# Chunked attention with a channel mix on one core: 1 KB rows for refetched weights, stores of pairs on another queue, a new order of all steps

## The chip, the cores and the metric

The kernel runs on one core of a Trainium2 chip. The metric is device time in microseconds of that core for one execution. TensorE multiplies, VectorE and ScalarE work on tiles in between, and DMAs are issued from the queues of SyncE (SP), ScalarE and GpSimd (POOL). A page of the hardware profiler and its trace belong to the kernel.

## What is computed

Attention runs in chunks of 64 rows within a sequence of 576, for 8 batches and 8 heads of width 64. Its result goes through a channel mix: each row is blended with the row before it by two vectors, and two matrix products with a squared ReLU between them are gated by a sigmoid.

```python
scores = scale * np.matmul(q_c, k_c.transpose(0, 1, 2, 4, 3))
attn = np.exp(scores - np.max(scores, axis=-1, keepdims=True))
out = np.matmul(attn / (np.sum(attn, axis=-1, keepdims=True) + 1e-09), v_c)
...
xk = mu_k * x + (1.0 - mu_k) * x_prev
xr = mu_r * x + (1.0 - mu_r) * x_prev
k = np.maximum(xk @ w_k, 0.0)
v = k * k @ w_v
r = 1.0 / (1.0 + np.exp(-(xr @ w_r)))
return (r * v).astype(np.float32)
```

There are 8 x 576 = 4608 rows of 512 channels; `w_k` is 512 x 1024, `w_v` 1024 x 512, `w_r` 512 x 512, all float32.

## The kernel before

The 4608 rows are cut into 18 groups of 256 rows, and each group into two tiles of 128. For each tile t the kernel loads q, k and v, brings q and k into a form with channels on partitions, and multiplies the scores (steps `S`, line 714). VectorE and ScalarE make the softmax (`S` or, from group 3 on, `Z` for a whole group), TensorE transposes it and multiplies with v (steps `P`, lines 831 and 844). The first three groups are loaded in natural rows (`load_nat`, lines 459 and 476) and turned on TensorE (`T`, lines 639 and 663). From group 3 on `load_blocks` (lines 519 and 521) fetches blocks of 32 x 32 (four DMAs for a step such as `bk11.2`), and VectorE transposes within them (`D`, line 689). `load_v` (line 491) takes four DMAs a tile.

The channel mix multiplies float32 values as a high and a low part, three passes each. The gates `R` (line 1130) take twelve matmuls of 512 columns a tile. Groups 0 to 3 multiply directly (`K`, line 1084, and `V`, line 1163). From group 4 on two groups form a pair (pairs 2 to 8) and go through a scheme with seven products of blocks instead of eight: `M` (line 1396, fourteen series of twelve matmuls of 256 columns) for the first product, `V1` to `V7` (line 1486, as many) for the second. ScalarE and VectorE move the results out, add them (`C`, line 1410), square them (`E`) and split them into high and low parts (`F`, line 1440); `O` (lines 1500 and 1504) adds and gates the second product, and `Q` stores a tile (line 1150).

The scheme needs sums of weights. Those of `w_v` (`tv`, eight pieces of 512 KB in sum form) and the split gate weights `wr` (four pieces) are made once, written to a buffer `kept` in HBM (lines 1282 and 1299), and fetched again for each of the pairs 3 to 8, because their places in SBUF are used for other tiles in between. `load_pair_weights` does that from POOL's queue: steps `L` (line 1308 for `tv`, line 1319 for `wr`), twelve DMAs of 512 KB a pair, each a row of 4 KB on each of 128 partitions.

Nothing is scheduled at run time. The functions only record named steps. `ORDER`, a table of 2089 words, lists the steps in the order in which they are issued, with the engine behind a colon where there is a choice (`:A` ScalarE, `:D` VectorE); `PLACE` gives every tile its offset in one of two arenas in SBUF or its bank in PSUM. The framework adds a semaphore wait wherever a step reads or overwrites what another engine or a DMA still works on. Each engine and each queue runs its own steps strictly in this order, so a step that waits holds all behind it on its engine. Eight semaphores serve the DMAs of each kind of queue in turn: a DMA of POOL also waits until the one eight before it has landed. SP issues everything but the refetches.

Of the kernel before, what the change touches and what calls it, by code (L numbers as in the profile page):

```python
# [19 lines left out]
G = 256  # L20
# [3 lines left out]
W.0:D swr1.0 cwr1.1:A cwr1.0:A W.1 nk0.0 nq0.0 mu.0 nk0.1 nq0.1 nq1.0 swk1.0 nk1.0 v0.0 v1.0 swr0.0  # L24
nk2.0 T0.6 T0.8:D mu.1 T0.0 mu.2:A T0.7:A cwr1.2:D T0.1:A T0.2:D T0.3 T0.9 S0.0 cwr1.3:D T0.11:D
T0.10:A T0.5:A T0.4:A S0.1:D S1.0 S0.2:D S1.1:D S1.2:D S0.3:A S0.4:D S0.5:D P0.3:D hwr1.0:A T1.0
P0.0 T1.3 cwk1.1:A S1.3:A P0.1:A cwk1.0:A S1.4:D S1.5:D P0.2 P0.4:D cwk1.2:D hwr1.1:D cwk1.3:D P1.0
T1.4:A T1.2:A P1.1:A T1.1:A dg.2 dg.3 Mr0.0 P1.2 S2.0 T1.5:A S3.0 T2.3 cwr0.1:A cwr0.0:A T2.5:A
T2.4:A hwk1.0:A P1.3:D Mr0.1:D P1.4:D Ak9.0:D S2.1:D cwr0.2:D Mr0.2:D cwr0.3:D S2.2:D Mr1.0 hwr0.0:A
nq2.0 T2.0 swk3.0 T2.1:A S2.3:A cwk3.0:A S3.1:D hwr0.1:D S3.2:D S3.3:A T2.2:A hwk1.1:D Mr1.1:A  # L30
cwk3.1:A dg.1 dg.0 Mk0.0 S2.4:D R00.0 Mk1.0 P2.3:D S3.4:D S2.5:D P2.0 S3.5:D Mr1.2:D cwk3.2:D
R00.1:A Mk0.1:A cwk3.3:D P2.1:D v3.0 v2.0 swk2.0 swk0.0 kr.0 cwk2.0:A cwk2.1:A P3.0 P3.1:A R01.0
cwk2.2:D Mk1.1:D hwk3.0:A hwk3.1:D Mk1.2:D cwk2.3:D P2.2 S4.0 P3.2 S5.0 P2.4:A R01.1:A cwk0.0:A
cwk0.1:A Mr2.0 hwk2.0:A Mr2.1:A Mk0.2:D cwk0.2:D S5.1:D Mk2.0 swv3.0 cwv3.0:A P3.3:D P3.4:A Mk2.1:A
hwk2.1:D Mr2.2:D cwk0.3:D Mk3.0:D K01.0 R10.0 bk4.3 swv2.0 bk4.0 swv1.0 bk4.1 hwk0.0:A K01.1:A
Mk2.2:D S4.1:D Mk3.1:D hwk0.1:D cwv3.1:A Mk3.2:D cwv3.2:D K03.0 K03.1:A R10.1:A cwv1.0:A K01.2:A
Mr3.0:D K00.0 K02.0 cwv3.3:D K01.3:A hwv3.0:D Mk3.3:D hwv3.1:D Mr3.1:D cwv1.1:A K00.1:D swv0.0
K00.2:A cwv0.0:A K03.2:A cwv1.2:D K01.4:D cwv1.3:D K13.0 K12.0 cwv0.1:A K03.3:D Mr3.2:D cwv0.2:D
cwv2.1:A cwv2.0:A cwv2.2:D cwv0.3:D bk4.2 K02.1:A K02.2:A hwv1.0:A hwv1.1:D R11.0 K00.3:A hwv0.0:A
K00.4:D hwv0.1:D S5.2:D D8.1:D Ar2.0:D K03.4:D K10.0 R11.1:A cwv2.3:D K10.1:A K13.1:A S5.3:A K02.3:A  # L40
K11.0 K02.4:D S4.2:D hwv2.0:D K13.2:D hwv2.1:D K10.2:A V01.0 V00.0 V01.1 V00.1 K13.3:D Ak2.0:D
S5.4:D V00.2 V01.2 V01.3 V01.4 V00.3 V01.5 V01.6 V01.7 V00.4 K10.3:A S4.3:A K11.1:A S4.4:D S4.5:D
K11.2:A K11.3:A K12.1:A K11.4:D S5.5:D K10.4:D P4.0 V00.5 V00.6 P5.0 V11.0 V00.7 V11.1 V10.0 V11.2
V11.3 U0.2:D U1.2:D U0.0:D bq4.0 bq3.2 bq3.3 bq3.0 bq3.1 D7.0:D K12.2:D bk3.0 v4.0 bk3.3 bk3.1 bk3.2
v5.0 U0.3:D K13.4:D D6.0:D K12.3:A P4.1:A P5.1:A D6.1:D V01.8:D D7.1:D K12.4:D U0.1:D U0.4:D S6.0
P4.2 P5.2 S7.0 Z3.0:D Ak2.2:A Bk2.1:D Z3.1:D V11.4 V10.1 Ak2.1:A Z3.2:A A2.0:A Hk12.0:A V00.8:D
# [294 lines left out]
def tile_chunk_attention_channel_mix(  # L341
# [76 lines left out]
    def queue(e):  # L418
        return nc.scalar if e == "A" else nc.sync
# [1197 lines left out]
```

## Time and profile before

| | |
|---|---|
| time, median of 3 runs | 666.2 us (665.04 to 672.01) |
| the profiled execution | 667.85 us |
| its span, first to last instruction | 666.0 us |
| mean granted clock of TensorE | 0.944 |
| DMA traffic | 93.35 MB, 139 GB/s over the span |

The profiled execution's own time stands 1.85 us above its span: what lies around the first and last instruction. In the rows below, times are microseconds from the start of the span unless marked ns. The number in brackets at the end of a timeline row is the idle time of the engine just before that row, and behind the arrow stands what ended it. DMA rows give the count, the size of one and the median time from issue to landing.

### The profile page before, as it was taken

How to read it: one execution, taken by the hardware profiler on the slowest of the kernel's cores; microseconds unless marked ns; L12 is line 12 of the kernel's file. 1: busy time of each engine (PE TensorE's matmuls, PEld its weight loads, DVE VectorE, ACT ScalarE, POOL GpSimd, SP SyncE). 2: the span in 40 equal slices, each digit the busy share in tenths (PEclk: the TensorE clock that was granted, in tenths of full speed). 3: DMA queues.
4: the chain of work that ended last, by engine and by line, in shares of the span. 5: the costliest groups of instructions: out<-in, count | busy, mean ns of one | idle time of the engine just before them, and what ended most of it. 6: DMA issues, size and time to landing. Idle time of an engine off the chain costs nothing. (4 is left out here: it accounts for less than half of the span.)

```text
span 666.0 us, 15832 instructions
## 1 busy us (share of the span) xinstructions
PE 589.9 (89%) x6183; PEld 544.3 (82%) x6183; DVE 526.5 (79%) x882; ACT 411.6 (62%) x811; POOL 52.4 (8%) x94
## 2 busy tenths in 40 slices
PE   6689899799988999879986959969998979999997
PEld 4578888688868998779875959959887879999897
DVE  4677799859798999779856857769879778998684
ACT  4486574545875996677644836547855846686451
POOL 4300000000000020002100201001100210011000
PEclk8789999979989999989997979979999979999999
DMA  9777532433344388536934675635746957233601
GB/s 244 170 197 225 154 66 51 109 75 58 101 99 81 85 276 237 140 76 169 295 58 115 154 178 160 179 62 135 222 87 169 246 163 181 78 127 84 234 1 64
DMA packets 200123, 93.35 MB, mean 140 GB/s; under 512 B 178024, under 2 KB 181104, under 8 KB 200048
## 3 DMA queue, kind: packets, MB, share of 16 engines
q1 hardware_dynamic: 189680, 54.58, 36.6%
q0 software_dynamic: 10368, 37.75, 17.2%
q8 instruction: 49, 0.80, 0.5%
q14 instruction: 26, 0.21, 0.1%
HBM read 76.55 MB, written 15.73 MB: 139 GB/s over the span
## 5 line engine op out<-in xcount | busy, mean ns | idle before, releaser
L1396 PE MATMUL m<-rounded 128*128 128x256 f32 x1176 | 152.0, 289 | 12.5 <-ACT plain L412 4.1
L1486 PE MATMUL o<-rounded 128*128 128x256 f32 x1176 | 153.1, 290 | 8.4 <-DVE rounded L1440 7.1
L1396 PEld LDWEIGHTS m<-rounded 128*128 128x128 f32 x1176 | 147.1, 196 | 15.8 <-ACT plain L412 5.1
L1486 PEld LDWEIGHTS o<-rounded 128*128 128x128 f32 x1176 | 148.4, 197 | 10.7 <-DVE rounded L1440 7.7
L412 ACT ACTIVATE rounded<-plain 128x512 fp32r<-128x512 f32 (+1 forms) x166 | 105.7, 662 | 38.1 <-PE pv L1163 8.4
L1130 PE MATMUL pr<-rounded 128*128 128x512 f32 x432 | 111.6, 412 | 4.0 <-DVE rounded L954 2.0
L1130 PEld LDWEIGHTS pr<-rounded 128*128 128x128 f32 x432 | 84.1, 200 | 22.9 <-DVE rounded L954 2.5
L1440 DVE TENSOR_TENSOR rounded<-plain,rounded 128x512 fp32r<-128x512 f32 x98 | 65.2, 684 | 16.8 <-PE m L1396 5.4
L1007 ACT ACTIVATE plain<-xps,mu 128x256 f32<-128x256 f32 x128 | 54.5, 489 | 30.3 <-PE xps L844 20.6
L689 DVE STREAM_TRANSPOSE plain<-plain 128x512 f32<-128x512 f32 x60 | 41.5, 701 | 34.1 <-DMA plain<-in_q 18.0
L1013 ACT ACTIVATE plain<-xps,mu 128x255 f32<-128x255 f32 (+3 forms) x176 | 62.3, 450 | 0.7 <-PE s L714 0.7
L1308 POOL DMA_DIRECT2D rounded<-kept x48 | 26.3, 554 | 308.8 <-PE o L1486 86.6
L412 ACT ACTIVATE plain<-m 128x512 f32<-128x512 f32 x42 | 24.5, 596 | 41.0 <-DMA out<-plain 14.1
L1024 DVE TENSOR_TENSOR plain<-plain 128x512 f32<-128x512 f32 x64 | 43.0, 680 | 7.0 <-ACT plain L1013 6.7
L1084 PEld LDWEIGHTS pk<-rounded 128*128 128x128 f32 x384 | 47.2, 192 | 1.2 <-ACT plain L1142 0.6
L1084 PE MATMUL pk<-rounded 128*128 128x256 f32 x384 | 47.8, 284 | 0.0
L1163 PE MATMUL pv<-rounded 128*128 128x512 f32 x192 | 47.5, 397 | 0.0
L844 PE MATMUL xps<-plain 64*64 64x64 f32 x1152 | 28.7, 236 | 17.3 <-DMA plain<-in_v 8.8
L844 PEld LDWEIGHTS xps<-plain 64*64 64x64 f32 x1152 | 23.8, 147 | 21.8 <-DMA plain<-in_v 10.9
L1163 PEld LDWEIGHTS pv<-rounded 128*128 128x128 f32 x192 | 35.5, 190 | 7.0
L1410 DVE TENSOR_TENSOR plain<-m,plain 128x512 f32<-128x512 f32 x42 | 28.3, 682 | 14.9 <-ACT plain L412 11.5
L1448 DVE TENSOR_TENSOR plain<-plain 128x512 f32<-128x512 f32 x56 | 38.0, 686 | 0.5
(103 smaller groups left out, 739.0 us busy)
## 6 DMA issues: line engine op xcount, KB each, us to landing
rounded<-kept POOLq DMA_DIRECT2D x72, 512.0 KB, 6.5
plain<-in_v SPq DMA_DIRECT2D x144, 64.0 KB, 2.4
out<-plain SPq DMA_DIRECT2D x36, 256.0 KB, 2.3
kept<-rounded SPq DMA_DIRECT2D x12, 512.0 KB, 2.8
plain<-in_q SPq DMA_DIRECT2D x160, 32.0 KB, 2.0
plain<-in_k SPq DMA_DIRECT2D x160, 32.0 KB, 2.1
plain<-in_moe_w_k SPq DMA_DIRECT2D x4, 1024.0 KB, 6.4
plain<-in_moe_w_v SPq DMA_DIRECT2D x4, 1024.0 KB, 5.7
```

Of the source, the lines that this page charges most:

```text
L412: nc.scalar.activation(to, x, AF.Copy)
L689: nc.vector.transpose(out=x, in_=x)
L844: nc.tensor.matmul(T[f"xps{g}"][halves[c], 2 * j + a, tl * TT + e * CH : tl * TT + (e + 1) * CH], T[f"v{t}"][halves[j], hp, e, :], T[f"pT{ ...
L1007: nc.scalar.activation(now(nm, h)[:, c], xps()[:, cb], AF.Copy, scale=mu2[:, 0, i, cb : cb + 1])
L1013: nc.scalar.activation(before(nm)[:, cb, s : s + n], xps()[:, cb, s - 1 : s - 1 + n], AF.Copy, scale=mu2[:, 1, i, cb : cb + 1],)
L1024: engine[e].tensor_tensor(now(nm, h), now(nm, h), before(nm)[:, 2 * h : 2 * h + 2], ALU.add)
L1084: nc.tensor.matmul(pk[:, e, :], wk_at(f // 4)[:, a, cb, f % 4 * P : (f % 4 + 1) * P], x[:, b, cb, :], start=(n == 0), stop=(n == 3 * NB - 1),)
L1130: nc.tensor.matmul(pr, xr_at(g, a, cb)[:, tl * TT : (tl + 1) * TT], wr_of(g, cb // 2)[:, b, cb % 2, :], start=(n == 0), stop=(n == 3 * NB ...
L1163: nc.tensor.matmul(pv, kk_at(g, a, f // 2)[:, f % 2, tl * TT : (tl + 1) * TT], wv_at(f // 4)[:, :, b, f % 4, :], start=(f == 0 and n == 0) ...
L1396: nc.tensor.matmul(ps[w][:, e, :], left(n, a, cb, 2 * u + e), right(g, n, b, cb), start=first and i == 0, stop=i == 11, skip_group_check=True,
L1440: engine[e].tensor_tensor(form(p, n, u, 1), r(i), f32(form(p, n, u, 0)), ALU.subtract)
L1486: nc.tensor.matmul(ps[w][:, tl, :], form(p, n, u, a)[:, e, tl * TT : (tl + 1) * TT], moving(n, b, 2 * u + e), start=first and i == 0, stop ...
```

## The change

Three things are edited in the code. A refetch of 512 KB is now issued as four DMAs, each of 256 columns, so a row of 1 KB on each of 128 partitions. The stores `Q` of pairs are issued from POOL, and the function `queue` knows POOL. The two tables are drawn anew: all steps are the same, but they stand in another order, some on the other of the two engines they may use, with other places. Twelve of the first loads are marked for ScalarE's queue in the new table.

```diff
     def queue(e):
-        return nc.scalar if e == "A" else nc.sync
+        return {"A": nc.scalar, "G": nc.gpsimd}.get(e, nc.sync)
...
+    def fetch(to, of):
+        for c in range(0, 1024, 256):
+            nc.gpsimd.dma_start(out=to[:, c : c + 256], in_=of[:, c : c + 256])
+
     def load_pair_weights(p):
...
                 def fn(e, n=n, u=u):
-                    nc.gpsimd.dma_start(
-                        out=tv_at(p, n, u).rearrange("p s c n -> p (s c n)"), in_=kept[2 * (n - 4) + u]
-                    )
+                    fetch(tv_at(p, n, u).rearrange("p s c n -> p (s c n)"), kept[2 * (n - 4) + u])
...
                 for h in range(2):
-                    nc.gpsimd.dma_start(out=x[:, 1024 * h : 1024 * (h + 1)], in_=kept[8 + 2 * i + h])
+                    fetch(x[:, 1024 * h : 1024 * (h + 1)], kept[8 + 2 * i + h])
...
                 do.task = f"Q{c}{tl}_{p}"
-                do(store(2 * p + c, tl), "Q")
+                do(store(2 * p + c, tl), "G")
```

Of the table of the order, its first line:

```diff
-W.0:D swr1.0 cwr1.1:A cwr1.0:A W.1 nk0.0 nq0.0 mu.0 nk0.1 nq0.1 nq1.0 swk1.0 nk1.0 v0.0 v1.0 swr0.0
+nq0.0:A nk0.0:A swr1.0 nk0.1:A mu.0 nq0.1:A W.0:D W.1 T0.0 T0.6 T0.2:D P0.3:D T0.1:D T0.8:D T0.7:D
```

**POOL's queue.** The rows below are those from the first refetch on, before the change (`rounded` is the arena that holds the split weights, `kept` the buffer in HBM; line 1319 fetches gate weights, line 1308 sums of `w_v`).

```order
L1319 DMA rounded<-kept 128x1024 x4
L1308 DMA rounded<-kept 128x1024 x7
L1319 DMA rounded<-kept 128x1024 x2
L1308 DMA rounded<-kept 128x1024 x2
L1319 DMA rounded<-kept 128x1024 x2
L1308 DMA rounded<-kept 128x1024 x5
```

After the change POOL has, from its first refetch on (line 1305 is the new `fetch`, line 1150 a store):

```order
L1305 DMA rounded<-kept 128x256 x16
L1150 DMA out<-plain 128x512
L1305 DMA rounded<-kept 128x256 x4
L1150 DMA out<-plain 128x512
L1305 DMA rounded<-kept 128x256 x4
L1150 DMA out<-plain 128x512 x2
L1305 DMA rounded<-kept 128x256 x44
L1150 DMA out<-plain 128x512 x3
```

The four stores of pair 2 now stand between the refetches of pair 3, and the stores of pair 3 behind its last refetch and the first ones of pair 4.

**SP's queue.** Around the loads of k for group 11 (line 519 loads its first 64 rows, line 521 the other 192), before the change:

```order
L491 DMA plain<-in_v 64x4x64 x4
L519 DMA plain<-in_k 32x4x32 x2
L521 DMA plain<-in_k 32x6x32 x4
...
L519 DMA plain<-in_k 32x4x32 x2
L521 DMA plain<-in_k 32x6x32 x4
L1150 DMA out<-plain 128x512
L491 DMA plain<-in_v 64x4x64 x4
L1150 DMA out<-plain 128x512 x2
L521 DMA plain<-in_k 32x8x32 x8
```

And at the same loads after it:

```order
L491 DMA plain<-in_v 64x4x64 x4
L519 DMA plain<-in_k 32x4x32 x2
L521 DMA plain<-in_k 32x6x32 x4
...
L521 DMA plain<-in_q 32x8x32 x12
L519 DMA plain<-in_k 32x4x32 x2
L521 DMA plain<-in_k 32x6x32 x4
L521 DMA plain<-in_q 32x8x32 x4
L491 DMA plain<-in_v 64x4x64 x8
```

The stores are gone from here, and loads for the next group are mixed in earlier.

**The start.** ScalarE's first steps before the change:

```order
L579 ACT_TABLE_LOAD
L579 ACTIVATE plain<-plain 128x1024
L575 ACTIVATE plain<-plain 128x1024
L540 ACTIVATE mu_78<-mu_t 128x8
L541 ACTIVATE mu_78<-mu_t 128x8
```

And after it:

```order
L476 DMA plain<-in_q 64x4x128 x2
L476 DMA plain<-in_k 64x4x128 x4
L476 DMA plain<-in_q 64x4x128 x2
L459 DMA plain<-in_q 128x8x64 x2
L575 ACT_TABLE_LOAD
L575 ACTIVATE plain<-plain 128x1024
L459 DMA plain<-in_k 128x8x64 x2
```

The natural loads of groups 0 and 1 (eight and four DMAs) have moved from SP's queue to ScalarE's, ahead of its first work but for two of them.

## Rows read from the trace of the kernel before

**Rows 1.** The page, part 1: busy us, share of the span, instructions of each engine.

```profile
PE 589.9 (89%) x6183; PEld 544.3 (82%) x6183; DVE 526.5 (79%) x882; ACT 411.6 (62%) x811; POOL 52.4 (8%) x94
```

**Rows 2.** The chain that ended last: start us, us, what.

```profile
623.95 11.78 PE m L1396 x96
635.73 2.75 PE pr L1130 x12
...
642.66 18.72 PE o L1486 x156
```

**Rows 3.** Groups by line: count, busy us, mean ns of one, idle before and its releasers.

```profile
L1396 PE MATMUL m<-rounded 128*128 128x256 f32 x1176 | 152.0, 289 | 12.5 <-ACT plain L412 4.1
L1486 PE MATMUL o<-rounded 128*128 128x256 f32 x1176 | 153.1, 290 | 8.4 <-DVE rounded L1440 7.1
```

**Rows 4.** TensorE's timeline, six gaps: start us, us, what, idle before it.

```profile
31.81 0.45 PE L663 MATMUL trk<-ident,plain 64*64 64x64 f32 x2 [4.48 <-DMA plain<-in_k]
...
132.59 0.33 PE L844 MATMUL xps<-plain 64*64 64x64 f32 x2 [2.97 <-DMA plain<-in_v]
...
351.87 1.43 PE L844 MATMUL xps<-plain 64*64 64x64 f32 x41 [5.50 <-ACT plain L412]
...
394.14 2.07 PE L1486 MATMUL o<-rounded 128*128 128x256 f32 x8 [7.11 <-DVE rounded L1440]
...
437.67 1.62 PE L714 MATMUL s<-plain 64*64 64x64 f32 x49 [4.07 <-ACT plain L412]
...
537.40 1.94 PE L831 MATMUL pt<-ident,plain 128*128 128x128 f32 x8 [5.37 <-DVE plain L803]
```

**Rows 5.** VectorE's timeline ahead of four of these gaps.

```profile
349.90 0.71 DVE L689 STREAM_TRANSPOSE plain<-plain 128x512 f32<-128x512 f32 x1 [6.74 <-DMA plain<-in_k]
...
392.47 0.71 DVE L689 STREAM_TRANSPOSE plain<-plain 128x512 f32<-128x512 f32 x1 [8.02 <-DMA plain<-in_q]
...
434.03 0.71 DVE L689 STREAM_TRANSPOSE plain<-plain 128x512 f32<-128x512 f32 x1 [4.39 <-DMA plain<-in_q]
...
534.83 0.71 DVE L689 STREAM_TRANSPOSE plain<-plain 128x512 f32<-128x512 f32 x1 [6.71 <-DMA plain<-in_k]
```

**Rows 6.** DMA from 520 to 540 us: POOL's queue (q0), issues and us to landing.

```profile
q0 software_dynamic: 1440, 5.24, 77.8%
...
rounded<-kept POOLq DMA_DIRECT2D x10, 512.0 KB, 6.5
...
plain<-in_k SPq DMA_DIRECT2D x5, 32.0 KB, 8.0
```

**Rows 7.** DMA of the whole run: rows and MB by queue, issues.

```profile
q1 hardware_dynamic: 189680, 54.58, 36.6%
q0 software_dynamic: 10368, 37.75, 17.2%
...
plain<-in_k SPq DMA_DIRECT2D x160, 32.0 KB, 2.1
```

**Rows 8.** The buffer `kept`: ns of one issue (min, median, max), us to landing.

```profile
L1308 POOL DMA_DIRECT2D rounded<-kept x48: 527/537/740, 243.6 to 618.0; - x48
...
DMA to landing us min/median/max: 2.7/6.3/12.1
```

**Rows 9.** SP's own waits: us in total, times, longest.

```profile
SPq L1150 <- DVE plain L1504: 86.6, 4, 41.3
```

**Rows 10.** Stores of the whole run: us to landing; ns of one issue.

```profile
out<-plain SPq DMA_DIRECT2D x36, 256.0 KB, 2.3
...
L1150 SPq DMA_DIRECT2D out<-plain x36: 332/432/602, 120.0 to 662.6; - x36
```

**Rows 11.** SP's timeline, natural loads of groups 0 and 1, first and last.

```profile
1.22 1.36 SPq L476 DMA_DIRECT2D plain<-in_k  x2
...
10.34 1.62 SPq L459 DMA_DIRECT2D plain<-in_k  x2
```

**Rows 12.** Waits of all engines: us in total, times, longest.

```profile
ACT plain L412 <- DMA out<-plain: 14.1, 4, 5.2
```

More of the change, by code (lines that the diff above doesn't have):

```diff
@@ L29 @@
[L29 to L34, printed above, removed]
@@ L196 @@
+O8.2:A V7_8.0 F3_81.0:A O8.3:D F3_81.1:D V7_8.1 V3_8.0 V3_8.1 O8.6:D O8.4:D O8.8:D O8.5:D O8.7:D
+V4_8.0 V4_8.1 O8.9:D Q00_8.0 Q01_8.0 Q10_8.0 Q11_8.0
 """
 PLACE = """
-idle:4096 warm:0 mu_t:2 diag_k0:15872 diag_k1:13824 diag_r0:11264 diag_r1:10752 natk0:15360
-natq0:14336 natk1:5632 natq1:4608 natk2:6656 natq2:14336 st_wr0:7680 st_wr1:0 st_wk0:3072
-st_wk1:2048 st_wk2:7168 st_wk3:0 st_wv0:3584 st_wv1:6656 st_wv2:8704 st_wv3:0 wr0:4096 wr1:0
-wk0:6144 wk1:10240 wv0:19456 wv1:24064 trq00_0:3 trq01_0:0 q0:13824 trq10_0:1 trq11_0:3 trk00_0:1
@@ L316 @@
-f411_8:9728 f510_8:5632 f511_8:33280 f710_8:37376 f711_8:36864 f610_8:25088 f611_8:24064
-f310_8:35840 f311_8:24576 o0_8:1 o11_8:13824 o1_8:2 o2_8:3 o22_8:13312 o12_8:14336
+idle:3072 warm:0 mu_t:1 diag_k0:4608 diag_k1:5120 diag_r0:6144 diag_r1:6656 natk0:0 natq0:15360
+natk1:9216 natq1:12288 natk2:14336 natq2:13312 st_wr0:10240 st_wr1:1024 st_wk0:7168 st_wk1:7168
+st_wk2:10240 st_wk3:1024 st_wv0:7680 st_wv1:4096 st_wv2:9728 st_wv3:1024 wr0:4096 wr1:0 wk0:6144
+wk1:10240 wv0:23552 wv1:18944 trq00_0:3 trq01_0:0 q0:13312 trq10_0:1 trq11_0:3 trk00_0:1 trk01_0:2
@@ new lines @@
+ak1_5:5632 br_5:8704 ar0_5:11776 ar1_5:8192 xr00_5:35840 xr10_5:34816 xr01_5:32256 xr11_5:36864
+raw3_2:7680 t30_2:29184 t31_2:36352 t10_2:28672 t11_2:23040 t20_2:26624 t21_2:25600 b220_2:14336
+b221_2:35328 t40_2:34304 t41_2:33792 pr_4_0:1 sg_4:9728 pr_4_1:0 pr_5_0:3 sg_5:3072 pr_5_1:2
+m0_2_0:2 c11_20:12288 m1_2_0:0 m2_2_0:3 c22_20:10752 c21_20:512 c12_20:8192 f100_2:36352
+f101_2:35328 f200_2:38912 f201_2:32256 f400_2:28672 f401_2:23040 f500_2:14336 f501_2:29696
+f700_2:33792 f701_2:35840 f600_2:32256 f601_2:34816 f300_2:35840 f301_2:38400 m0_2_1:1 c11_21:0
@@ new lines @@
+c12_40:9728 f100_4:36352 f101_4:36864 f200_4:36352 f201_4:35328 f400_4:14336 f401_4:34816
+f500_4:30720 f501_4:36864 f700_4:36864 f701_4:32256 f600_4:1024 f601_4:35840 f300_4:1024
+f301_4:37888 m0_4_1:0 c11_41:15360 m1_4_1:2 m2_4_1:1 c22_41:4608 c21_41:14848 c12_41:12288
+f110_4:36352 f111_4:37376 f210_4:32256 f211_4:35840 f410_4:23040 f411_4:1536 f510_4:31232
+f511_4:37376 f710_4:31744 f711_4:37376 f610_4:29184 f611_4:38400 f310_4:1024 f311_4:34304 o0_4:1
+o11_4:9216 o1_4:2 o2_4:0 o22_4:6144 o12_4:12800 k10:9216 q10:5120 v20:9216 v21:6144 p_10:14336
@@ new lines @@
+f610_5:23040 f611_5:14336 f310_5:36352 f311_5:23040 o0_5:2 o11_5:13312 o1_5:1 o2_5:3 o22_5:12800
+o12_5:3072 k12:7680 q12:5120 v24:9216 v25:14336 p_12:1536 pT24:11776 pT25:2048 bk_12:1024
+ak0_12:12288 ak1_12:2560 xk_12:32256 br_12:5632 ar0_12:13824 ar1_12:2048 xr00_12:38400 xr10_12:38912
+xr01_12:14336 xr11_12:36864 k13:2560 q13:13312 v26:10240 v27:5632 p_13:0 pT26:14848 pT27:14336
+bk_13:14336 ak0_13:11776 ak1_13:10240 br_13:4608 ar0_13:13312 ar1_13:14848 xr00_13:35328
+xr10_13:32256 xr01_13:33280 xr11_13:23040 raw3_6:12800 t30_6:29184 t31_6:34816 t10_6:23040
@@ new lines @@
+c22_61:10752 c21_61:2048 c12_61:2560 f110_6:34304 f111_6:37888 f210_6:14336 f211_6:34304
+f410_6:36864 f411_6:37376 f510_6:38400 f511_6:33792 f710_6:36352 f711_6:33792 f610_6:33792
+f611_6:27648 f310_6:38400 f311_6:36352 o0_6:3 o11_6:12800 o1_6:0 o2_6:1 o22_6:10752 o12_6:11264
+k14:7168 q14:4608 v28:13824 v29:6656 p_14:13824 pT28:14336 pT29:13312 bk_14:15360 ak0_14:13312
+ak1_14:5120 xk_14:25600 br_14:9216 ar0_14:1536 ar1_14:6656 xr00_14:23040 xr10_14:38912 xr01_14:14336
+xr11_14:34304 k15:9216 q15:3584 v30:10240 v31:4608 p_15:13824 pT30:2048 pT31:3072 bk_15:5632
@@ new lines @@
+f400_7:37376 f401_7:31744 f500_7:39424 f501_7:30720 f700_7:14336 f701_7:33280 f600_7:33280
+f601_7:39424 f300_7:32256 f301_7:31232 m0_7_1:0 c11_71:10240 m1_7_1:3 m2_7_1:2 c22_71:15872
+c21_71:4608 c12_71:11776 f110_7:38912 f111_7:30208 f210_7:23040 f211_7:37888 f410_7:34816
+f411_7:29696 f510_7:35840 f511_7:23040 f710_7:32768 f711_7:38400 f610_7:38912 f611_7:32256
+f310_7:37888 f311_7:23040 o0_7:1 o11_7:14336 o1_7:0 o2_7:2 o22_7:15872 o12_7:10240 k16:5632 q16:8192
+v32:8192 v33:8704 p_16:14336 pT32:14336 pT33:14848 bk_16:5120 ak0_16:12800 ak1_16:13824 xk_16:26624
@@ new lines @@
+br_16:12288 ar0_16:13312 ar1_16:15360 xr00_16:28672 xr10_16:26112 xr01_16:14336 xr11_16:29184
+k17:11776 q17:0 v34:9216 v35:9728 p_17:8192 pT34:8192 pT35:8704 bk_17:11776 ak0_17:15872
+ak1_17:13312 br_17:9216 ar0_17:15872 ar1_17:15360 xr00_17:25600 xr10_17:18432 xr01_17:23040
+xr11_17:32256 raw3_8:14848 t30_8:32768 t31_8:33280 t10_8:28672 t11_8:31744 t20_8:14336 t21_8:25600
+b220_8:29184 b221_8:27648 t40_8:31744 t41_8:28672 wr0_8:0 wr1_8:4096 tv50_8:33280 tv51_8:8192
+tv60_8:29696 tv61_8:6144 tv70_8:26112 tv71_8:17408 tv40_8:34304 tv41_8:30720 pr_16_0:3 sg_16:8192
@@ new lines @@
+pr_16_1:0 pr_17_0:0 sg_17:10752 pr_17_1:3 m0_8_0:1 c11_80:14336 m1_8_0:3 m2_8_0:0 c22_80:12288
+c21_80:15360 c12_80:15872 f100_8:28160 f101_8:27136 f200_8:35840 f201_8:36864 f400_8:32768
+f401_8:29184 f500_8:35328 f501_8:18432 f700_8:35328 f701_8:32256 f600_8:36352 f601_8:37376
+f300_8:33792 f301_8:33280 m0_8_1:2 c11_81:13312 m1_8_1:0 m2_8_1:3 c22_81:11776 c21_81:14848
+c12_81:12800 f110_8:27648 f111_8:28672 f210_8:38400 f211_8:36352 f410_8:31744 f411_8:16896
+f510_8:32256 f511_8:28672 f710_8:37888 f711_8:35840 f610_8:36864 f611_8:19968 f310_8:32256
@@ L318 @@
+f311_8:35328 o0_8:0 o11_8:13824 o1_8:3 o2_8:1 o22_8:14336 o12_8:13312
 """
```

519 lines of the change are left out of this document (241 added, 278 removed).

## The prediction

> **What bounds the kernel now.** I read the page first. TensorE works 589.9 of 666.0 us [rows 1], the other engines less, and the chain that ends last is TensorE alone from 623.95 to 661.38 us [rows 2]. So the time is TensorE's work, its idle 666.0 - 589.9 = 76.1 us, and what a lower clock costs. Second, the price of one matmul in three unbroken series at full clock [rows 2]: 11.78 / 96 = 0.123 us (a pair's first product), 18.72 / 156 = 0.120 us (its second), 2.75 / 12 = 0.229 us (gates). All matmuls of the two products would take 1176 x (0.123 + 0.120) = 285.8 us; they were busy 152.0 + 153.1 = 305.1 us [rows 3]. So 19.3 us there are work at a lower rate: the granted clock averages 0.944, part of the time at 1.2 instead of 2.4 GHz. That is 19.3 / 76 = 0.25 us of slow work per us idle for these two lines alone; I use 0.3, between 0 and 0.45.
>
> Third, TensorE's timeline, for its gaps [rows 4]: 4.48 us before 31.81 for a load of k, 2.97 before 132.59 for v, 5.50 before 351.87, 7.11 before 394.14, 4.07 before 437.67, 5.37 before 537.40. The last four name ScalarE or VectorE. VectorE's timeline says what stood behind [rows 5]: its transposes of loaded blocks waited 6.74, 8.02, 4.39 and 6.71 us for k or q, each ending 1.6 to 3.7 us before the gap of TensorE does. So 4.5 (head), 16.6 (394, 437, 537) and 8.5 (132, 351), 30 of 76 us idle, come from loads that land late; small gaps of the kind I leave out. The page itself does not say this: it lists the nearest engine.
>
> Fourth, why they are late. From 520 to 540 us ten refetches of 512 KB hold 77.8% of the DMA engines, and the loads of k issued there take 8.0 us to land [rows 6]; over the whole run such loads take 2.1 [rows 7]. POOL offers 512 KB every 0.54 us [rows 8], more than the engines move, so loads stand behind refetches. The gap at 394 follows refetches in the same way. The one at 351 does not: there SP itself came late to its loads.
>
> **The change part by part.** *Rows of 1 KB.* 72 refetches become 72 x 4 = 288, 48 per pair for six pairs. One issue takes 0.537 us, 0.527 to 0.740 [rows 8]; it still has 128 rows, so I take 0.54, with these ends as bounds. POOL then issues for 156 instead of 39 us, 26 us per pair. A pair has 28 series of twelve (28 x 1.46 = 41 us) and four gates (11 us), 52 us before any attention, so 26 fit. What is offered falls to 128 KB / 0.54 us = 243 GB/s. What a row of 1 KB costs an engine no row shows. The queues' means are 17.2% x 666 x 16 / 10368 = 177 ns for 3.6 KB and 36.6% x 666 x 16 / 189680 = 21 ns for 0.29 KB [rows 7]; a line through them gives 55 ns, my value; the bounds are 44 (a quarter of 177) and 177. At 55 the 8 rows that each engine gets from one issue take 0.44 of 0.54 us: a fifth stays free, and a load waits behind 55 ns where it waited behind 177. Of the 16.6 us I take two thirds, -11.0; bounds 0 and -16.6.
>
> The Trainium skill, page "DMA: Bandwidth & Descriptors", section "SWDGE vs HWDGE vs iDMA", says that an engine changes queues only between packets and that a packet is preferably up to 4096 B, so it may hold several rows. By that the short rows need not let loads in sooner and only the slower offer helps; the trace cannot tell, since it counts rows. What it would give is the second rival.
>
> *Stores of pairs on POOL.* 28 issues leave SP for POOL, where they also wait for the gated sums. SP's waits for these look large, 86.6 us in 4, the longest 41.3 [rows 9]; but the long ones stand behind SP's last load, with nothing queued, so I count no gain. What is queued now behind a waiting store is refetches: the order shows pair 2's stores between refetches of pair 3. By program order no refetch is left less than 6 us of TensorE's work between its issue and the first matmul that needs it, counted at 0.54 us an issue, as before the change. Cost 0 while landing stays below that: 512 KB took 2.7 to 12.1 us, 6.3 in the middle [rows 8], and these carry a quarter. At the very end the four last stores leave from POOL: an issue costs 0.54 instead of 0.43, and landing was 2.3 [rows 10]; +0.6, between 0 and 4.
>
> The Trainium skill, page "SBUF — State Buffer", section "Who interferes with whom", says that VectorE's copies in a two-port mode shut POOL out, so that DMAs issued there starve. It speaks against moving anything to POOL. The trace does not bear it out: the longest of the 48 issues is 0.740 us [rows 8] in a run where VectorE is busy 79% [rows 1]. It is the last rival.
>
> *Order anew: the head.* Twelve loads of q and k go to ScalarE's queue; they held SP for 8.5 us from 1.22 to 11.96 us (the first and the last of six rows stand in [rows 11]). ScalarE's first work waits for the first weight load anyway. The loads of group 2 come that much sooner, ahead of the second loads of v as well: -4.5; bounds 0 and -8.5.
>
> *Order anew: SP.* Ahead of the last q or k load of group 11 SP has 488 issues instead of 496, of group 13 584 instead of 627, of group 14 648 instead of 670, while TensorE's work ahead of their scores stays within 3 us. At 0.43 us an issue [rows 10] that is 3 to 18 us of room. Of the 8.5 us I take half, -4.2; bounds 0 and -8.5.
>
> *Places anew.* ScalarE waited 14.1 us for stores that still read a place [rows 12], and a part of it reached TensorE. I take -2, between -6 and +6 (stores on POOL may sit longer).
>
> *The new order's own waits.* 76 - 30 = 46 us of idle are mostly waits among engines, which another order puts elsewhere; no row shows them. An equally good order gives 0, one that trades them for earlier loads more: an eighth, +6, between -8 and +30.
>
> Sum of idle: -4.5 - 11.0 - 4.2 - 2 + 6 = -15.7; with 0.3 us of slow clock each -20.4; with the tail -19.8 us. 666.0 - 19.8 = 646.2 us of span. The profiled execution took 667.85, 1.85 above its span and 1.65 above the median of 666.2: 646.4, so 646 us.
>
> **The rivals.**
> *All late loads vanish* (chance 0.10). For it: loads outside refetches land in 2 us. Against: the gaps at 132 and 351 have no refetch beside them. -4.5 - 16.6 - 8.5 - 2 + 6 = -25.6, x 1.3 = -33: 634 us; 626 if the order's own waits stay as they were.
> *Only pacing* (0.11). The rows interleave no finer, just the lower offer helps: a third of 16.6 instead of two, 5.5 x 1.3 = 7 us more, 653.
> *Nothing left* (0.10). The waits pass to VectorE and ScalarE, whose chains stand right behind the loads: own waits +22 instead of +6, 667 us. For it: VectorE is busy 79%. Against: in the four gaps it had itself stood idle for a load.
> *Refetches late: slower* (0.14). If a row of 1 KB costs over 100 ns, eight take over 0.8 us, and the DMA engines, not POOL, set the pace: the 16 issues that stand last before a pair's second product fall behind 16 x 0.26 = 4 us, and landing takes 12 instead of 6, 10 us in all. 6 are covered, 4 are not: 24 us for six pairs, and the 11.0 are not gained: -15.7 + 11 + 24 = 19.3, x 1.3 = 25: 692 us. From some 7 us late per pair it is slower than before. Against: the line gives 55 ns.
> *POOL locked out* (0.03). Each issue waits for one VectorE instruction of 0.7 us: 48 x 1.24 = 60 us, longer than a pair without its attention. With 4 us uncovered per pair again 692 us. Against: rows 8.
>
> **How the numbers follow.** The forecast has 0.52 and holds 632 to 660. A measurement of this kernel tells about 1% from no change, 659.5 to 672.9. Faster: 0.50 of the forecast, 0.10 of the first rival, 0.07 of the second: 0.67. Same: 0.02, 0.04, 0.10 and a little of the fourth: 0.17. Slower: the rest, 0.16. The range 618 to 671 leaves out some 0.05 below (the bounds of -16.6 and of -8 together) and 0.15 above, the two slow rivals.
>
> **What would show it.** Right: TensorE idle near 60 us with a clock above 0.944; loads of k that land in 2 to 4 us while refetches run; POOL near 180 us busy at 0.54 us per issue; the gap at 31.8 us gone. Wrong: TensorE waiting for refetched weights; issues above 0.8 us; or loads on time and TensorE still idle 76 us, which would be the order's own waits.

## The result and the profile after

The changed kernel took 619.56 us (median of 4 runs, 618.28 to 619.9) beside 667.01 us for the kernel before in the same session: ratio 0.927, 95% interval 0.922 to 0.933, so 7% faster. The forecast was 646 us. Direction and range held; the gain came out at 47 us instead of 20.

The page of after, part 1 (busy us, share of the span and instructions of each engine), and its part 5 (groups by line: count, busy us, mean ns of one, idle before):

```profile
span 618.1 us, 16168 instructions
...
PE 571.4 (92%) x6183; PEld 529.1 (86%) x6183; DVE 531.3 (86%) x898; ACT 400.4 (65%) x793; POOL 186.3 (30%) x338
...
L1305 POOL DMA_DIRECT2D rounded<-kept x288 | 155.5, 551 | 340.2 <-DMA plain<-in_q 189.1
L1488 PE MATMUL o<-rounded 128*128 128x256 f32 x1176 | 152.3, 288 | 9.8 <-DVE rounded L1442 4.6
...
L1398 PE MATMUL m<-rounded 128*128 128x256 f32 x1176 | 149.0, 286 | 7.1 <-DVE rounded L1366 4.9
...
L1130 PE MATMUL pr<-rounded 128*128 128x512 f32 x432 | 102.6, 391 | 0.0
```

TensorE's idle time went from 76.1 us [rows 1] to 618.1 - 571.4 = 46.7, its busy time from 589.9 to 571.4 with the same 6183 matmuls. So 29.4 us of the gain are idle time and 18.5 are matmuls that took less time. The granted clock, as a mean over the run, rose from 0.944 to 0.971. The two products took 301.3 us where they took 305.1 [rows 3].

The largest gaps of TensorE that are left (timeline: start us, us, what, idle before it in brackets):

```profile
19.62 1.13 PE L663 MATMUL trq<-ident,plain 64*64 64x64 f32 x32 [3.15 <-ACT mu L541]
...
305.86 2.64 PE L1488 MATMUL o<-rounded 128*128 128x256 f32 x12 [3.53 <-DVE plain L1502]
...
364.39 5.76 PE L1488 MATMUL o<-rounded 128*128 128x256 f32 x34 [3.44 <-DVE rounded L1442]
...
463.44 2.72 PE L1398 MATMUL m<-rounded 128*128 128x256 f32 x11 [3.45 <-DVE rounded L1366]
```

None reaches 4 us; before, the six of [rows 4] stood between 2.97 and 7.11. Still, VectorE's waits for loads have hardly shrunk. The waits of after (us in total, times, longest):

```profile
DVE plain L689 <- DMA plain<-in_q: 20.1, 9, 4.4
...
DVE plain L689 <- DMA plain<-in_k: 7.5, 2, 5.4
...
DVE plain L689 <- DMA plain<-in_v: 3.4, 1, 3.4
```

That is 31.0 us in twelve waits, the longest 5.4. Before it was 33.7 in eight, the longest 8.0 (the four of [rows 5] are among them). The longest went, the sum hardly did, so this sum alone does not say how long TensorE stands idle. The wait of ScalarE for stores [rows 12] has no row in after at all.

### The profile page after: what moved, and what is told of

It reads as the page before. It is cut to its first block, busy times and chain, and to the rows that moved or that the text cites. A ratio compares the mean times of both kernels' runs of the same rounds, so it can differ in the third digit from the quotient of the medians.

```text
span 618.1 us, 16168 instructions
## 1 busy us (share of the span) xinstructions
PE 571.4 (92%) x6183; PEld 529.1 (86%) x6183; DVE 531.3 (86%) x898; ACT 400.4 (65%) x793; POOL 186.3 (30%) x338
## 3 DMA queue, kind: packets, MB, share of 16 engines
q0 software_dynamic: 43712, 45.11, 29.7%
## 5 line engine op out<-in xcount | busy, mean ns | idle before, releaser
L1305 POOL DMA_DIRECT2D rounded<-kept x288 | 155.5, 551 | 340.2 <-DMA plain<-in_q 189.1
L1488 PEld LDWEIGHTS o<-rounded 128*128 128x128 f32 x1176 | 146.3, 194 | 13.1 <-DVE rounded L1442 5.4
L1398 PE MATMUL m<-rounded 128*128 128x256 f32 x1176 | 149.0, 286 | 7.1 <-DVE rounded L1366 4.9
L1398 PEld LDWEIGHTS m<-rounded 128*128 128x128 f32 x1176 | 144.7, 193 | 9.3 <-DVE rounded L1366 5.4
L412 ACT ACTIVATE rounded<-plain 128x512 fp32r<-128x512 f32 (+1 forms) x145 | 93.1, 667 | 44.0 <-PE o L1488 9.9
L1130 PE MATMUL pr<-rounded 128*128 128x512 f32 x432 | 102.6, 391 | 0.0
L1130 PEld LDWEIGHTS pr<-rounded 128*128 128x128 f32 x432 | 79.7, 188 | 16.3 <-DVE rounded L954 0.5
L689 DVE STREAM_TRANSPOSE plain<-plain 128x512 f32<-128x512 f32 x60 | 41.5, 701 | 32.7 <-DMA plain<-in_q 20.1
L1073 ACT ACTIVATE plain<-plain 128x512 f32<-128x512 f32 x64 | 39.6, 633 | 17.3 <-DVE plain L1065 16.6
L1150 POOL DMA_DIRECT2D out<-plain x28 | 15.6, 557 | 69.4 <-DVE plain L1506 22.0
L414 DVE CAST rounded<-plain 128x512 fp32r<-128x512 f32 (+1 forms) x82 | 35.1, 432 | 1.0 <-PE pr L1130 0.2
```

Of the source, the lines that this page charges most:

```text
L412: nc.scalar.activation(to, x, AF.Copy)
L689: nc.vector.transpose(out=x, in_=x)
L1130: nc.tensor.matmul(pr, xr_at(g, a, cb)[:, tl * TT : (tl + 1) * TT], wr_of(g, cb // 2)[:, b, cb % 2, :], start=(n == 0), stop=(n == 3 * NB ...
L1305: nc.gpsimd.dma_start(out=to[:, c : c + 256], in_=of[:, c : c + 256])
L1398: nc.tensor.matmul(ps[w][:, e, :], left(n, a, cb, 2 * u + e), right(g, n, b, cb), start=first and i == 0, stop=i == 11, skip_group_check=True,
L1488: nc.tensor.matmul(ps[w][:, tl, :], form(p, n, u, a)[:, e, tl * TT : (tl + 1) * TT], moving(n, b, 2 * u + e), start=first and i == 0, stop ...
```

## The experiments

The change has three parts, so the first six kernels build the cube: old or new tables, rows of 4 KB or 1 KB, stores of pairs on SP or on POOL. "Loads" is the sum of VectorE's waits for q, k and v (L689). "Stores" is the sum of all waits for a store that still reads its place, on VectorE and ScalarE. Both are from the list of waits of each profiled run; idle is span minus TensorE's busy time. The time of before in the table is that of the session that held most of these runs, and each ratio is to the runs of before on the same chip. These runs of before had medians of 664.3 to 667.0 us from chip to chip, so a few us between two rows of different chips are judged by the ratios. Line numbers differ by one to seven between the kernels.

| kernel | tables, rows, stores | us | ratio to before (95%) | span | busy | idle | loads | stores |
|---|---|---|---|---|---|---|---|---|
| before | old, 4 KB, SP | 666.6 | | 666.0 | 589.9 | 76.1 | 33.7 | 21.6 |
| old_stores_pool | old, 4 KB, POOL | 656.0 | 0.988 (0.980 to 0.995) | 655.4 | 585.9 | 69.5 | 34.5 | 9.9 |
| old_rows1k | old, 1 KB, SP | 631.0 | 0.944 (0.939 to 0.950) | 630.5 | 582.9 | 47.6 | 12.3 | 12.6 |
| old_both | old, 1 KB, POOL | 627.8 | 0.945 (0.937 to 0.953) | 627.9 | 580.3 | 47.6 | 8.5 | 9.9 |
| order_alone | new, 4 KB, SP | 668.0 | 1.004 (0.9995 to 1.008) | 665.3 | 581.1 | 84.2 | 37.7 | 70.8 |
| new_rows4k | new, 4 KB, POOL | 650.2 | 0.973 (0.968 to 0.978) | 649.0 | 579.9 | 69.1 | 56.9 | 0 |
| new_stores_sp | new, 1 KB, SP | 642.7 | 0.961 (0.954 to 0.967) | 641.7 | 577.5 | 64.2 | 26.7 | 59.2 |
| after | new, 1 KB, POOL | 619.6 | 0.927 (0.922 to 0.933) | 618.1 | 571.4 | 46.7 | 31.0 | 0 |

**The order alone, and the three parts one at a time.** order_alone puts both edits back, new_rows4k the first, new_stores_sp the second:

```diff
-        for c in range(0, 1024, 256):
-            nc.gpsimd.dma_start(out=to[:, c : c + 256], in_=of[:, c : c + 256])
+        nc.gpsimd.dma_start(out=to, in_=of)
...
-                do(store(2 * p + c, tl), "G")
+                do(store(2 * p + c, tl), "Q")
```

> The new tables (order, places, head loads on ScalarE) with neither code edit: refetches in rows of 4 KB as one DMA of 512 KB, stores of pairs on SP. Theory 'rows' (the short rows of 1 KB carry at least half of the 47 us): 640 to 650 us, with gaps behind late loads of k and q again. Theory 'order' (the new order carries most of it): 620 to 630 us, with few such gaps though loads beside refetches still land late, because they are asked for earlier.

> The changed kernel with refetches in rows of 4 KB again (72 DMAs of 512 KB); stores stay on POOL. Theory 'rows': 640 to 650 us. Theory 'order': below 630 us. With the run of the order alone it also tells what the stores' queue is worth with long rows: my prediction says nothing, under 3 us.

> The changed kernel with the stores of pairs back on SP, rows of 1 KB kept. My prediction and both theories: within 4 us of 619.6. Rival theory 'stores' (a store that waits on SP holds the loads behind it): 630 us or more, with SP waiting tens of us for gated sums ahead of loads.

The new tables by themselves change nothing that can be measured (668.0 us, 1.004), which neither theory had: in the profiled runs TensorE's idle time grows by 8.1 us and its busy time falls by 8.8. With either edit they gain some, with both 47 us. new_rows4k came out at the upper end of what theory 'rows' said, new_stores_sp as theory 'stores' said. Waits of order_alone:

```profile
SPq L1150 <- DVE plain L1505: 109.5, 4, 55.1
...
ACT plain L412 <- DMA out<-plain: 36.8, 3, 22.0
...
PE pt L831 <- ACT plain L412: 20.0, 1, 20.0
```

The third row is one gap of TensorE of 20 us, behind a ScalarE that waits for a store. new_stores_sp shows how that comes about, step by step. Its timelines (SP, VectorE, TensorE; SP's rows are DMA issues):

```profile
328.26 5.26 SPq L491 DMA_DIRECT2D plain<-in_v  x8
333.62 7.83 SPq L521 DMA_DIRECT2D plain<-in_k  x16
341.56 1.83 SPq L1150 DMA_DIRECT2D out<-plain  x4
...
443.15 0.86 SPq L519 DMA_DIRECT2D plain<-in_k  x2
460.08 0.36 SPq L1150 DMA_DIRECT2D out<-plain  x1
460.48 2.03 SPq L521 DMA_DIRECT2D plain<-in_k  x4
```

```profile
323.66 0.69 DVE L1506 TENSOR_TENSOR plain<-plain 128x512 f32<-128x512 f32 x1
...
345.15 0.17 DVE L997 TENSOR_TENSOR plain<-last,mu 128x4 f32<-128x4 f32 x1 [12.41 <-DMA out<-plain]
...
483.00 0.71 DVE L689 STREAM_TRANSPOSE plain<-plain 128x512 f32<-128x512 f32 x1 [9.87 <-DMA plain<-in_k]
```

```profile
346.59 1.94 PE L831 MATMUL pt<-ident,plain 128*128 128x128 f32 x8 [12.20 <-DVE plain L803]
```

The last gated sum of pair 2 is ready at 324.35. SP does not issue the stores until 341.56, because its loads of v and k stand ahead of them in its order. VectorE, which needs a store's place, waits 12.41 us, and TensorE behind it 12.20. The other direction stands at 444: a store waits there 16.1 us for its sum (444.01 to 460.08), the loads of k are queued behind it, SP then issues without a longer pause until 483.31, and VectorE waits 9.87 us for k, until 483.00. So in one queue stores stand behind loads that are early, and loads behind stores that are late. In after two stores are issued 0.4 us behind the sum that ends at 319.6 (POOL's timeline), and the last at 323.52, behind four refetches:

```profile
320.02 1.19 POOL L1150 DMA_DIRECT2D out<-plain  x2 [2.23 <-DVE plain L1506]
```

The waits for stores fall from 59.2 us to 0 and the time by 23.1 us. That is what the stores' move is worth in the new tables; with rows of 4 KB it is 17.8 (668.0 to 650.2).

**The two edits on the old tables.** The old ORDER and PLACE, with one edit or both:

```diff
+    def fetch(to, of):
+        for c in range(0, 1024, 256):
+            nc.gpsimd.dma_start(out=to[:, c : c + 256], in_=of[:, c : c + 256])
...
-                do(store(2 * p + c, tl), "Q")
+                do(store(2 * p + c, tl), "G")
```

> The old tables with refetches in rows of 1 KB (288 DMAs), stores on SP. Theory 'rows': 640 to 650 us, and the waits of VectorE for blocks of k and q near 392 and 535 us shrink from 8.0 and 6.7 us to below 3. Theory 'order': 658 to 667 us, the gap goes elsewhere.

> The old tables with only the stores of pairs on POOL, rows of 4 KB. My prediction said nothing for it: 662 to 668 us. Theory 'stores': 645 to 655 us, as with the new tables (668.0 to 650.2).

> The old tables with both code edits: rows of 1 KB and stores of pairs on POOL. It splits the 11 us between rows alone with old tables (631.0) and the changed kernel (619.6). Theory 'tables': the new tables earn them, so 628 to 632 us. Theory 'stores': the stores' queue earns them with any tables, so 612 to 622 us.

Rows of 1 KB alone give 35.6 us, in the old order, and nothing else is touched there; that is more than theory 'rows' said. On the other three edges of the cube they give 28.2 (old tables, stores on POOL), 25.4 (new, SP) and 30.6 (new, POOL). The parts depend on each other and do not add up to the 47. Waits of old_rows1k, and part 3 of its page (rows and MB by queue, share of 16 engines):

```profile
DVE plain L689 <- DMA plain<-in_q: 8.4, 5, 3.4
...
DVE plain L689 <- DMA plain<-in_k: 3.9, 2, 2.1
```

```profile
q0 software_dynamic: 41472, 37.77, 25.9%
```

VectorE's waits for q and k fall from 33.7 to 12.3 us, and TensorE's idle falls by 28.5. Queue q0 carries only refetches here, so it gives the time of one of its packets: 25.9% x 630.5 x 16 / 41472 = 63 ns. These are 288 x (128 + 16) packets: beside the 128 rows of a DMA 16 more are counted. For each row it is 71 ns.

On the old tables stores on POOL give 10.7 us with long rows by the medians and 8 by the ratio, whose interval reaches from 3 to 13, so the size is uncertain; the waits for stores fall from 21.6 to 9.9 us. With short rows they give 3.2 us by the medians and nothing by the ratios (0.944 and 0.945), and TensorE's idle time is 47.6 us in both: no gain is shown there. With both edits, the tables then give 8.2 us more by the medians, 12 by the ratios (0.945 to 0.927). So theory 'tables' was the nearer one for this last step.

**Row length or pacing?** Short rows are also more issues, so POOL offers 243 GB/s where it offered 980. Three kernels take the two apart, all with the new tables and stores on POOL: new_quarters issues four DMAs of 32 partitions with 4 KB rows, new_rows2k two with 2 KB rows, and new_4k_paced one of 512 KB with twelve memsets of a tile that nobody reads behind it.

```diff
-        for c in range(0, 1024, 256):
-            nc.gpsimd.dma_start(out=to[:, c : c + 256], in_=of[:, c : c + 256])
+        for c in range(0, 128, 32):                        # new_quarters
+            nc.gpsimd.dma_start(out=to[c : c + 32], in_=of[c : c + 32])
+        for c in range(0, 1024, 512):                      # new_rows2k
+            nc.gpsimd.dma_start(out=to[:, c : c + 512], in_=of[:, c : c + 512])
+        nc.gpsimd.dma_start(out=to, in_=of)                # new_4k_paced
+        for _ in range(12):
+            nc.gpsimd.memset(pause, 0.0)
```

> The changed kernel with each 512 KB refetch cut by partitions instead of by columns: four DMAs of 32 partitions, rows of 4 KB, still 128 KB a DMA and 288 DMAs. Theory 'row length' (a load waits behind one long row on its engine): as with rows of 4 KB, 642 to 652 us. Theory 'pacing' (POOL offers less per issue and eight DMAs in flight are 1 MB instead of 4): 618 to 626 us, if an issue still takes about 0.5 us; the issue time with 32 rows is read from the trace.

> The changed kernel with rows of 2 KB (two DMAs of 256 KB for a refetch). Theory 'row length': half of the gain lost, 630 to 640 us. Theory 'pacing': 256 KB per 0.54 us is 485 GB/s, more than the engines move, so nearly all of it lost, 643 to 650 us.

> The changed kernel with rows of 4 KB in DMAs of 512 KB, and behind each of them twelve small memsets on POOL into a tile of their own that nothing reads, so that POOL offers less per us without shorter rows. Theory 'pacing': 618 to 628 us, if the memsets take 1.2 us or more together. Theory 'row length': 645 to 652 us, as without them (650.2).

| kernel | row | one DMA, every | offered GB/s | us | ratio (95%) | loads |
|---|---|---|---|---|---|---|
| new_rows4k | 4 KB | 512 KB, 0.535 us | 980 | 650.2 | 0.973 (0.968 to 0.978) | 56.9 |
| new_quarters | 4 KB | 128 KB, 0.497 us | 264 | 640.0 | 0.964 (0.957 to 0.972) | 45.8 |
| new_rows2k | 2 KB | 256 KB, 0.535 us | 490 | 634.9 | 0.955 (0.945 to 0.964) | 42.2 |
| new_4k_paced | 4 KB | 512 KB, 3.4 us | 154 | 631.5 | 0.951 (0.945 to 0.956) | 29.5 |
| after | 1 KB | 128 KB, 0.54 us | 243 | 619.6 | 0.927 (0.922 to 0.933) | 31.0 |

The intervals are from the medians of the issue, or for new_4k_paced from its POOL timeline:

```profile
294.48 0.54 POOL L1305 DMA_DIRECT2D rounded<-kept  x1 [0.20 <-issue]
295.01 2.47 POOL L1307 MEMSET pause<- 128x64 f32 x12
297.94 0.53 POOL L1305 DMA_DIRECT2D rounded<-kept  x1 [0.45 <-PE o L1490]
```

Pacing alone, with rows and DMAs as long as before, recovers 650.2 - 631.5 = 18.7 of the 30.6 us, or 15 of 30 by the ratios: it helps by itself. Of the theories, new_4k_paced came out between both, new_quarters just below and new_rows2k within what 'row length' said. For the row length itself the evidence is weaker. New_quarters and after offer nearly the same, and short rows are 20.4 us better; 2 KB rows at twice the offer are still 5 us better than 4 KB rows in quarters. But a quarter also touches 32 partitions instead of 128, and that was not free: POOL's queue, refetches and stores, held the 16 DMA engines for 20.9% x 649.0 = 136 us in new_rows4k and for 30.7% x 640.7 = 197 us in new_quarters, with rows of the same length, and for 29.7% x 618.1 = 184 us in after. And new_4k_paced brings VectorE's waits for loads as low as after has them (29.5 and 31.0), while TensorE waits 5.7 us for v and 2.3 for weights, where after has 0.5 and 0. So no kernel here changes the row length and nothing else; that short rows do more than pace is likely and not shown.

The prediction weighed a rule of the Trainium skill here ("DMA: Bandwidth & Descriptors", section "SWDGE vs HWDGE vs iDMA"): an engine changes queues between packets, and a packet may hold several rows. If several short rows shared a packet here, their length would give nothing and new_quarters would run like after. It was 20 us slower, which speaks against that; with the 32 partitions it does not settle it.

**One DMA with short rows.** `kept` laid out so that one DMA of 512 KB has 512 rows of 1 KB: short rows without the many issues.

```diff
-        for c in range(0, 1024, 256):
-            nc.gpsimd.dma_start(out=to[:, c : c + 256], in_=of[:, c : c + 256])
+        nc.gpsimd.dma_start(out=to.rearrange("p (c n) -> p c n", c=4), in_=short(of))
```

> The changed kernel with the kept buffer laid out in four blocks of 256 columns, so that one DMA of 512 KB has 512 rows of 1 KB: short rows with 72 issues instead of 288. Theory 'row length': 617 to 624 us however much POOL offers. Theory 'pacing': if an issue stays near 0.6 us, 640 to 650 us; if it grows with the rows to 2 us, as fast as the changed kernel.

It took 671.1 us (667.13 to 676.84 in 10 runs; ratio 1.010, 1.006 to 1.014), about 1% above before. Its POOL timeline and its waits:

```profile
540.47 0.74 POOL L1310 DMA_DIRECT2D rounded<-kept  x1 [4.36 <-issue]
544.92 0.75 POOL L1310 DMA_DIRECT2D rounded<-kept  x1 [3.71 <-issue]
```

```profile
POOL rounded L1310 <- issue: 138.1, 34, 5.2
...
PE o L1493 <- DMA rounded<-kept: 22.0, 8, 5.8
...
PE pr L1130 <- DMA rounded<-kept: 13.3, 3, 4.7
...
DVE plain L689 <- DMA plain<-in_q: 9.9, 5, 3.3
```

POOL idles about 4 us between two such issues though nothing that the profile shows holds it: one DMA every 4.4 us here, 119 GB/s. VectorE waits less for loads (19.1 us for q, k and v together), and the weights come late: TensorE waits 35.3 us for them. The stores, on the same queue, come late as well: ScalarE and VectorE wait 34.1 us for them, where after has no such wait. Both theories missed. Late weights are the prediction's rival "Refetches late: slower", here because POOL pauses and not because rows are dear. In this kernel refetches can be too dense and too thin. Why POOL idles there was not tested, and at 119 GB/s the run says nothing on the row length.

**The head.** The twelve first loads go back from ScalarE's queue to SP's; all else is as in after:

```diff
-nq0.0:A nk0.0:A swr1.0 nk0.1:A mu.0 nq0.1:A W.0:D W.1 T0.0 T0.6 T0.2:D P0.3:D T0.1:D T0.8:D T0.7:D
-nq1.0:A cwr1.0:A mu.1 nk1.0:A mu.2:A cwr1.1:A S0.0 S0.1:D T0.9 T0.3 T0.10:D T0.11:A T0.4:A T0.5:A
+nq0.0 nk0.0 swr1.0 nk0.1 mu.0 nq0.1 W.0:D W.1 T0.0 T0.6 T0.2:D P0.3:D T0.1:D T0.8:D T0.7:D
+nq1.0 cwr1.0:A mu.1 nk1.0 mu.2:A cwr1.1:A S0.0 S0.1:D T0.9 T0.3 T0.10:D T0.11:A T0.4:A T0.5:A
```

> The changed kernel with the twelve natural loads of groups 0 and 1 on SP's queue instead of ScalarE's, in the new order. My prediction priced the move at 4.5 us idle, 6 us with the clock: 623 to 630 us. Rival: the head is held by the landing of its first megabytes, not by issuing, so within 2 us of 619.6.

It took 614.0 us (611.98 to 615.33; ratio 0.923, 0.918 to 0.928): 5.5 us less than after by the medians, the lowest of all, but 2.7 by the ratios, whose intervals overlap. ScalarE's timeline in after, then in new_head_sp, each with TensorE's first gates behind it:

```profile
2.12 7.92 ACTq L476 DMA_DIRECT2D plain<-in_k  x4
...
14.61 1.28 ACT L575 ACT_TABLE_LOAD   x1 [14.61 <-DMA plain<-in_k]
...
19.32 0.18 ACT L540 ACTIVATE mu<-mu_t 128x8 f32<-128x8 f32 x1 [2.30 <-issue]
...
39.85 3.02 PE L1130 MATMUL pr<-rounded 128*128 128x512 f32 x12
```

```profile
0.72 1.28 ACT L575 ACT_TABLE_LOAD   x1 [0.72 <-PEq L1601]
...
11.77 0.15 ACT L540 ACTIVATE mu<-mu_t 128x8 f32<-128x8 f32 x1
...
37.23 3.00 PE L1130 MATMUL pr<-rounded 128*128 128x512 f32 x12
```

On ScalarE's queue the loads hold ScalarE itself: it loads its table at 14.61 instead of 0.72 and moves the blend vectors at 19.32 instead of 11.77. TensorE's gap at 19.62 (above) waits for just that. The first gates start 2.6 us later for it. That much the head explains; the profiled spans differ by 4.6 us, and the rest arises behind 300 us, where the order of both is the same. Why was not tested. The prediction had the move as a gain; it is a loss.

**Slower offer on top.** new_head_sp with one such memset behind each DMA:

```diff
         for c in range(0, 1024, 256):
             nc.gpsimd.dma_start(out=to[:, c : c + 256], in_=of[:, c : c + 256])
+            nc.gpsimd.memset(pause, 0.0)
```

> The fastest kernel so far (head loads back on SyncE's queue, 614.0 us) with one small memset on GpSimd behind each refetch DMA of 1 KB rows, so that 128 KB are offered about every 0.75 us where it was 0.54. If what is left of VectorE's waits for q, k and v (26.7 us of idle) comes from how densely the refetches are offered, the waits shrink to 10 to 18 us and the time is 606 to 612. If the row length has already given all there was, the time stays at 612 to 616. If the weights now come late, TensorE waits for 'rounded<-kept' and the time is above 618.

It took 614.5 us (ratio 0.922, 0.915 to 0.929), the same. But the offer fell less than planned. Its POOL timeline:

```profile
321.31 0.56 POOL L1306 DMA_DIRECT2D rounded<-kept  x1
321.84 0.19 POOL L1307 MEMSET pause<- 128x64 f32 x1
321.93 0.56 POOL L1306 DMA_DIRECT2D rounded<-kept  x1
```

The memset runs partly beside the next issue, so a DMA leaves every 0.62 us and not every 0.75. VectorE's waits for loads are 30.9 us (15.1, 12.2 and 3.6 for q, k and v), no fewer than the 26.7 without it. An offer 13% lower buys nothing here; whether a much lower one would, stays open.

## Why the prediction was right or wrong

**What failed.** Two terms of the sum, first of all. Rows of 1 KB were sized at -11.0 us of idle and gave -28.5 on the old tables and -20.0 on the new ones. Stores on POOL were put at nothing ("so I count no gain") and gave -17.5 in the order that the change has. On the path tables, rows, stores through the cube (order_alone, new_stores_sp, after) TensorE's idle time moves by +8.1, -20.0 and -17.5, together -29.4; the sum had -4.7 (head, SP, places and own waits), -11.0 and 0, together -15.7.

**Right.** The bound: TensorE with its idle time, and a part of that idle is loads that come late behind dense refetches. One issue costs 0.54 us (median 0.537, longest 0.925) and POOL is busy 186.3 us, 180 foreseen. A packet of short rows takes 63 ns, or 71 for each row (55 foreseen, 100 was the point where it would turn). No weight comes late in after. The gap at 31.8 us is gone. POOL is not locked out, with VectorE busy 86%. In the dense stretch of after from 320 to 340 us POOL's queue holds 82.0% of the engines, near the 0.44 of 0.54 us foreseen, and loads of k (16 KB here) take 4.1 us to land, at the edge of the 2 to 4 of the text; loads of q take 5.7:

```profile
q0 software_dynamic: 3674, 3.91, 82.0%
...
plain<-in_k SPq DMA_DIRECT2D x17, 16.0 KB, 4.1
...
plain<-in_q SPq DMA_DIRECT2D x5, 32.0 KB, 5.7
```

**Mis-sized: rows of 1 KB, two thirds of 16.6 us.** On the old tables they took 28.5 us off TensorE's idle, more than the outer bound of 16.6. The mechanism was right, the bound was not: it was made of three large gaps (394, 437, 537) and left out "small gaps of the kind". VectorE's list of waits held 33.7 us for loads of q and k, and 21.4 of them went; in TensorE's own list the waits for ScalarE fell from 26.2 to 9.1 us, those for VectorE from 25.1 to 15.8. The sum of VectorE's waits for loads would not have been a safe measure either: after keeps 31.0 of it and still loses 29.4 us of idle.

**Wrong: stores on POOL, "with nothing queued, so I count no gain".** They gave 23.1 us on the new tables and 17.8 with rows of 4 KB. On the old tables they gave 8 to 11 with long rows and nothing that is shown with short ones, so the step fails for the change as a whole, where the order moves loads ahead of the stores. The step read only SP's waits for stores [rows 9] and asked what is queued behind them. It did not ask what the store itself stands behind. A row that hints at it was at hand [rows 12]: ScalarE waited 14.1 us for stores. The prediction put that down to places, -2; with the stores on POOL and the old places it is 5.1.

**Wrong in sign: the head, "-4.5; bounds 0 and -8.5".** Its gap of 4.48 us went, and ScalarE's late start put others in its place: with the loads back on SP the first gates start 2.6 us sooner. The step counted the time that SP gains and took ScalarE for free, because its "first work waits for the first weight load anyway". The table load and the blend vectors don't.

**SP's order, places and own waits, -4.2 -2 +6.** They cannot be taken one by one. The tables together gave nothing with neither edit and 8 to 12 us with both. With the stores on SP the waits for them are large, 70.8 us in order_alone. That is how loads moved ahead pay: the stores behind them come later. It needs the second queue.

**The slow clock, 0.3 us per us of idle.** With the same tables it was right: old_rows1k lost 28.5 us of idle and 589.9 - 582.9 = 7.0 us of busy time, 0.25 per us. But the new tables also shorten the busy time: old_both and after are alike in idle (47.6 and 46.7) and 8.9 us apart in busy. Most of it is in the gates, 110.1 us in old_both, 102.6 in after (L1130, 432 matmuls). Their lines in before and after (ns of one, min, median, max):

```profile
L1130 PE MATMUL pr<-rounded x432: 387/390/794, 41.1 to 642.3; 128*128 128x512 f32 x144
...
L1130 PE MATMUL pr<-rounded x432: 387/389/497, 39.8 to 591.8; 128*128 128x512 f32 x144
```

The typical gate is the same, and the difference is the slow clock. In before 31 gate matmuls took over 600 ns, in old_both 23, with the new tables none. In before they stand near 50, 84, 138 and 367 us, behind gaps of TensorE of 2.30, 2.03, 2.97 and 4.04 us; from 136.0 to 140.5 the granted clock is 0.50, which is 1.2 GHz. With the new order no gate is that slow: the longest takes 497 ns. The prediction had no term for which work falls into the slow clock.

The sum of idle was -15.7 and is -29.4: 13.7 us more, 17 with the slow clock, and with the gates' 9 that is the difference between 646 and 620. Of the rivals, "All late loads vanish" (634, or 626) was nearest in the number, not in the mechanism, since 31.0 us of such waits are left. "Only pacing" (653) lies 33 us above the result, though pacing is a part of the gain.

## What to carry to other kernels

Where bulk prefetches run beside small urgent loads, try them in smaller pieces and issued no faster than they drain; test row length and pacing apart, since pacing alone gave 15 to 19 of 31 us here. In a queue that runs strictly in order, ask of every instruction both what stands behind it and what it stands behind: a store that is late in the queue holds its place in memory and so the engines that need it. Don't bound a gain by the gaps that are large enough to see: three of them held 16.6 us here, and the edit took 28.5. And when the order changes, look which work falls into stretches of the slow clock.

## What the runs showed of the hardware

- A row of 1 KB took 71 ns of a DMA engine in old_rows1k, a row of 4 KB 17.2% x 666.0 x 16 / 9216 = 199 ns in before, each with its share of the 16 further packets of a DMA: a byte costs some 40% more in the short row, and yet the kernel gained 36 us. These times hold waiting too: from 320 to 340 us in after the shares of the two large queues are 82.0% and 37.7%, more than 100% together.
- A DMA of 512 rows issued from POOL takes 0.75 us to issue but was followed by about 4 us in which POOL did nothing (138.1 us in 34 such waits), while DMAs of 128 rows follow each other at 0.54.
- The Trainium skill ("DMA: Bandwidth & Descriptors", section "Issuing engines are not separate DMA queues") says that issuing from several engines saves only the time to initiate the DMA. The 28 stores at about 0.43 us make 12 us of that; moving them gave 23.1. The waits for stores fell from 59.2 us to 0: they no longer stood behind SP's loads and held none back.
